# Block-sparse attention with a gated feed-forward on one Trainium2 core: the later Q, K, V casts move from GpSimd to ScalarE and VectorE, over one stage buffer

## The chip, the cores and the metric

The kernel runs on one core of one Trainium2 chip. The time is the device's, in microseconds (us): before the change the median of three runs is 315.1 us, from 315.01 to 315.33. TensorE is written PE in the profile, its weight loads PEld, VectorE is DVE, ScalarE is ACT, GpSimd is POOL, and SyncE, which here only issues transfers, is SP. A `q` behind an engine's name is its queue's sequencer.

## The reference

The inputs are q, k and v of 4 batches x 8 heads x 768 positions x 64, a list of 3 sampled key blocks for each of 24 query blocks, and the weights of a feed-forward layer from 512 to 1536 and back. All are fp32. The attention is masked by blocks of 32 positions; its output, with the heads side by side, is the input of a layer with an RMS norm and a SiLU gate.

```python
scores = scale * np.matmul(q, k.transpose(0, 1, 3, 2))
# a block pair is kept if |i - j| <= 1, if i or j is the first or last block,
# or if j is one of the three sampled blocks of i
scores = np.where(mask, scores, -1e9)
attn = softmax(scores)
x = np.matmul(attn, v)               # (4, 8, 768, 64) -> (3072, 512)
xn = x / rms(x) * rms_g
out = (silu(xn @ w_gate) * (xn @ w_val)) @ w_out
```

## The kernel before

**Tiling.** The 3072 positions are cut into 12 chunks of 256, three for each batch. Attention of a chunk is 12 tiles: four head pairs by three groups of 256 keys. A tile is four score matmuls (L556) into a PSUM bank pair `s`, one exponential on ScalarE into a third of the P buffer `pt` (L571), one multiplication with the 0/1 mask on VectorE (L578), and eight matmuls with V (L592). V has a column of ones behind it, so that these also give the softmax's denominator. A `pt` buffer holds the three tiles of one head pair, and there are four such buffers. In chunk 0 (`PEMASK`) the mask is added on TensorE instead (L562).

After a head pair VectorE divides by the denominator (`o_norm`, L604 and L606) into `x1`. After four pairs ScalarE sums squares (L615), GpSimd makes the reciprocal root (`rs`, L621 and L623), and VectorE scales into the bf16 `x2` (L628). The chunk must then be turned, so that its features lie on partitions, as `xn`. For chunks 0 and 11 this is done by eight transposes on TensorE and a copy from PSUM (`x_transposes` L638, `x_copy` L644). For chunks 1 to 10 (`XDMA`) it is two transposing DMAs on SP's queue (`x_dma`, L651).

The feed-forward of a chunk has six steps. In each, TensorE makes 256 columns of gate and of value for two feature tiles (`gp`, `vp`, L757), ScalarE takes a tanh (`th`, L763), and VectorE makes two products (`uu` L767, `hp` L774). Then TensorE multiplies with w_out (`yp`, L784), ScalarE copies the result (L801), and SP stores it (L802). The last ten steps take their PSUM banks from those that the scores had, and are called `gv`.

**How Q, K and V come in.** Batch 0's Q and K are cast to bf16 by the DMA or from small fp32 tiles, and transposed on TensorE. For batches 1 to 3, K, Q and V are loaded one after the other as fp32 into a `stage` tile of 1.5 MB (`load_stage`, L224, a DMA issued by GpSimd). There are two such tiles. GpSimd casts K and Q in six pieces of 512 columns each (`cast_c`, L229) and V in four pieces of 768 (`cast_v`, L234; batch 0's V too). The bf16 Q and K are then turned by transposing DMAs on SP's queue (L427), five for a batch, into `qkT`, from which the scores read.

**What sets the order.** No scheduler runs on the chip: each engine takes its instructions in the order in which they were emitted, and waits on semaphores. The order is made when the kernel is built, by a greedy planner (`Plan.run`, L50). Each task has the engines that may do it with a cost in us, the tasks that it depends on, buffers that it takes (`acq`) and gives back (`rel`), and a priority. At every step the planner takes the task with the smallest key, L98:

```python
key = (round(eager + wait + SOFT * t["prio"], 3), start + dur, t["seq"])
```

`wait` is `HOLD` for a task whose gate is closed. Only the scores have a gate: a score tile `i` is held while `i` is above `LEAD + SPEED * 144 * (share of feed-forward work done)`, and from tile 24 on, where tiles go in pairs, while the second `s` buffer isn't about to come free. A task that may run on two engines goes where its key is smaller. A transfer is reckoned as a share of one common DMA time, at L116, for the loads, and as a fixed latency for the transposing DMAs. The field `after` is a time before which the planner doesn't place a task; nothing in the emitted program enforces it. Loads of batch 2 have `after` 100, of batch 3 160.

Of the kernel before, what the change touches and what calls it, by code (L numbers as in the profile page):

```python
# [14 lines left out]
SEM = 0.06  # L15
START = dict(DVE=3.4, POOL=1.7, ACT=2.5, PE=4.4)
DMA0 = 3.0
HOLD = 0.2
SOFT = 0.0125
LEAD = 27  # L20
SPEED = 1.0
PRIO = {'av': 4, 'e': 10, 'g': 2, 'h': 6, 'm': 9, 'mk': 9, 'mt': -1, 'on': 3, 'rs': 2, 's': 2, 'sc': -12, 'sq': -7, 'th': -9, 'uu': 7, 'v': 4, 'x': 0, 'xt': -1, 'y': 7, 'yo': 1}


class Plan:
# [8 lines left out]
        self.tokens[name] = [0.0] * n  # L34

    def add(self, name, engines, fn, deps=(), prio=5, acq=(), rel=(), mode=None, lat=0.12,
            dma=None, after=0.0, gate=None, work=0.0):
        self.seq += 1
        assert name not in self.tasks, name
        self.tasks[name] = dict(  # L40
            name=name, engines=engines, fn=fn, deps=list(deps),
            prio=PRIO.get(name.split("_")[0].rstrip("0123456789"), prio), acq=list(acq),
            rel=list(rel), mode=mode, lat=lat, dma=dma, after=after, gate=gate, work=work,
            seq=self.seq)

    def soon(self, name, n):
# [3 lines left out]
    def run(self, log=None):  # L50
# [84 lines left out]
def kernel(  # L135
# [29 lines left out]
    const = ctx.enter_context(tc.tile_pool(name="const", bufs=1))  # L165
    raw = ctx.enter_context(tc.tile_pool(name="raw", bufs=1))
    qkpool = ctx.enter_context(tc.tile_pool(name="qkpool", bufs=2))
    ppool = ctx.enter_context(tc.tile_pool(name="ppool", bufs=4))
    xpool = ctx.enter_context(tc.tile_pool(name="xpool", bufs=2))
    work = ctx.enter_context(tc.tile_pool(name="work", bufs=2))  # L170
    ffw = ctx.enter_context(tc.tile_pool(name="ffw", bufs=3))
# [12 lines left out]
        return ps_f.tile([P, 512], FP32, name=name, tag="f")  # L184

    PEMASK = (0,)
    MAT = (0, 21.0, 32.0)
    QAT = (4.6, 20.0, 31.0)
    plan = Plan()
    for name, n in (("s", 2), ("o", 1), ("f", 3), ("pt", 4), ("x1", 2), ("x2", 3), ("xn", 3),  # L190
                    ("hp", 2), ("th", 3), ("uu", 3), ("yo", 3), ("qk", 2), ("raw", 1), ("sw", 8), ("stage", 2), ("t", 4)):
        plan.pool(name, n)

    kf = raw.tile([P, 2, NC * D], FP32, name="kf")
# [23 lines left out]

    stages = {}

    def load_stage(b, i):
        stages[b, i] = raw.tile([P, H, NC * D], FP32, name="stage", tag="stage", bufs=2)
        if b:
            nc.gpsimd.dma_start(out=stages[b, i], in_=(qv, kv, vv)[i][b])  # L224

    def cast_c(b, i, c):
        raw_tiles(b)
        flat = (qraw, kraw)[i][b].rearrange("p h w -> p (h w)")
        nc.gpsimd.tensor_copy(  # L229
            out=flat[:, c * DM:(c + 1) * DM].rearrange("p (h d) -> p h d", h=H),  # L230
            in_=stages[b, i][:, :, c * D:(c + 1) * D])

    def cast_v(b, pr):
        nc.gpsimd.tensor_copy(  # L234
            out=va[b % 2][:, 2 * pr:2 * pr + 2, :, 0:D],
            in_=stages[b, 2][:, 2 * pr:2 * pr + 2, :].rearrange("p h (c d) -> p h c d", c=NC))

    tid = const.tile([32, S], I32, name="tid")
# [74 lines left out]
    def act(n):  # L313
        return n / 1200.0 + 0.055
# [12 lines left out]
    def load_v0(lo):  # L327
        if lo == 0:
            load_stage(0, 2)
        nc.gpsimd.dma_start(out=stages[0, 2][:, lo:lo + 4, :], in_=vv[0, :, lo:lo + 4, :])  # L330
# [170 lines left out]
    for b in range(1, B):  # L501
        plan.add(f"rawq{b}", {"SP": 0.0}, lambda e: None, acq=["raw"], lat=0.0, prio=0,
                 deps=[f"raw{b - 1}"])
        for i in (1, 0, 2):
            swdge(f"l{b}_{i}", lambda b=b, i=i: load_stage(b, i), 4.4,
                  [">wo"] if (b, i) == (1, 1) else [">" + last], 20 + b, acq=["stage"],
                  after=0.0 if b == 1 else 60.0 * b - 20.0)
            last = f"l{b}_{i}"
            if i < 2:
                prev = None  # L510
                for c in range(NC):
                    plan.add(f"c{b}_{i}_{c}", {"POOL": 0.56}, lambda e, b=b, i=i, c=c: cast_c(b, i, c),
                             deps=[f"l{b}_{i}", f"rawq{b}"] + ([">" + prev] if prev else []),
                             rel=["stage"] if c == NC - 1 else [], prio=10)
# [109 lines left out]
        mss[ch] = rs  # L624

    def scale_x(ch, qt):
        x2s[ch, qt] = xpool.tile([P, DM], BF16, name="x2", tag="x2", bufs=3)
        nc.vector.scalar_tensor_tensor(  # L628
            out=x2s[ch, qt], in0=x1s[ch][:, qt].rearrange("p h d -> p (h d)"),
            scalar=mss[ch][:, qt:qt + 1], in1=gB, op0=ALU.mult, op1=ALU.mult)  # L630
# [9 lines left out]
                    in_=x2s[ch, qt][:, c * P:(c + 1) * P], identity=ident)  # L640

    def x_copy(e, ch):
        xns[ch] = xpool.tile([P, KC, CQ], BF16, name="xn", tag="xn", bufs=3)
        (nc.scalar.copy if e == "ACT" else nc.vector.tensor_copy)(  # L644
            out=xns[ch].rearrange("p c t -> p (c t)"),
            in_=xts[ch].rearrange("p c t -> p (c t)"))

    def x_dma(ch, qt):
        if qt == 0:
            xns[ch] = xpool.tile([P, KC, CQ], BF16, name="xn", tag="xn", bufs=3)  # L650
        nc.sync.dma_start_transpose(  # L651
            out=xns[ch][:, :, qt * P:(qt + 1) * P], in_=x2s[ch, qt])
# [53 lines left out]
    for ch in range(NCH):  # L706
# [178 lines left out]
```

## Time and profile before

| | |
|---|---|
| median of three runs | 315.1 us (315.01 to 315.33) |
| profiled execution: time, span | 314.4 us, 312.6 us |
| mean granted TensorE clock | 0.989 |
| busy: TensorE, VectorE, ScalarE, GpSimd | 291.9, 238.3, 214.4, 70.7 us |
| chain that ended last | TensorE 60%, VectorE 16%, DMA 8%, ScalarE 7%, GpSimd 5% |
| moved by DMA | 36.68 MB, mean 117 GB/s |

The span runs from the first to the last instruction of one profiled execution; its own time is 1.8 us longer. Busy times are unions of instruction records, and a matmul's record is longer than its share of the pipeline. "<-" behind a group of instructions names what ended the idle time before it. The columns of each view are told where it is shown.

### The profile page before, as it was taken

Reading aid. Unit: us, or ns where it says so; the run is one execution under the profiler, and the core shown is the slowest. Engines: PE = TensorE matmul, PEld = TensorE weight load, DVE = VectorE, ACT = ScalarE, POOL = GpSimd, SP = SyncE. Lnnn points to the kernel's source line nnn. Section 1 sums busy time; section 2 is a strip of 40 time slices with the busy share of each in tenths; the row PEclk is TensorE's granted clock in tenths of the full one; section 3 lists DMA queues with packets and bytes.
Section 4 is the critical chain, followed back from the end, with each engine's and each line's share of the span. In section 5 each row is a group of like instructions: output and inputs, shape, how many; then the busy total and the mean of one; then the engine's idle time right before and its main releaser. Section 6 shows DMA issues by size and latency. Waiting matters only on the chain.

```text
span 312.6 us, 7944 instructions
## 1 busy us (share of the span) xinstructions
PE 291.9 (93%) x3358; PEld 204.3 (65%) x3358; DVE 238.3 (76%) x439; ACT 214.4 (69%) x302; POOL 70.7 (23%) x108
## 2 busy tenths in 40 slices
PE   7697997799999497999999999999999999999995
PEld 2475675477757274875775875876866867858682
DVE  6238999779959478786996998887887887866361
ACT  4979997458797385767786776787787777733231
POOL 9551009350021009431002409420010010010000
PEclk9999999799999889999999999999999999999999
DMA  8999995893009702992107915954003003000001
GB/s 124 293 209 209 208 359 147 258 145 76 0 37 291 182 2 67 272 168 67 37 2 241 293 24 157 235 66 103 2 3 101 2 2 101 3 36 34 35 34 67
DMA packets 44135, 36.68 MB, mean 117 GB/s; under 512 B 31364, under 2 KB 37652, under 8 KB 44100
## 3 DMA queue, kind: packets, MB, share of 16 engines
q0 software_dynamic: 9984, 21.76, 27.5%
q1 hardware_dynamic: 33700, 14.16, 20.9%
q8 instruction: 26, 0.43, 0.6%
q10 hardware_dynamic: 416, 0.26, 0.3%
q14 instruction: 9, 0.07, 0.1%
HBM read 28.57 MB, written 6.29 MB: 112 GB/s over the span
## 4 chain that ended last, share of the span: by engine, by line
PE 60%; DVE 16%; DMA 8%; ACT 7%; POOL 5%; issue 4%; POOLq 0%; ACTq 0%; DVEq 0%
PE yp L784 14%; PE gp L757 13%; PE vp L757 12%; DVE pt L578 6%; PE gv L757 4%; DVE x L628 4%; DMA stage<-in_v_dram 4%; DMA xn<-x 4%; ACT junk L615 3%; ACT pt L571 3%; DVE uu L767 2%; DVE hp L774 2%; POOL rs L623 2%; DVE x L606 2%; ACT th L763 1%
## 5 line engine op out<-in xcount | busy, mean ns | idle before, releaser
L578 DVE TENSOR_TENSOR pt<-pt,Mk 128x1024 bf16<-128x1024 bf16 x132 | 94.5, 742 | 3.9 <-ACT pt L571 3.8
L784 PE MATMUL yp<-wo,hp 128*128 128x512 bf16 x288 | 71.5, 384 | 0.7 <-DVE hp L774 0.7
L757 PE MATMUL gp<-xn,wg 128*128 128x256 bf16 x512 | 67.3, 275 | 4.6 <-DMA xn<-x 4.6
L757 PE MATMUL vp<-xn,wv 128*128 128x256 bf16 x512 | 69.2, 272 | 0.1
L757 PEld LDWEIGHTS <-wg 128*128 128x128 bf16 x576 | 56.3, 98 | 14.3 <-DMA xn<-x 4.8
L592 PEld LDWEIGHTS <-pt 128*128 128x128 bf16 x1152 | 45.9, 98 | 28.3 <-DVE pt L578 11.1
L763 ACT ACTIVATE th<-gp 128x512 bf16<-128x512 f32 x64 | 38.2, 597 | 37.4 <-PE gp L757 37.1
L767 DVE SCALAR_TENSOR_TENSOR uu<-th,gp 128x512 bf16<-128x512 bf16 x64 | 43.6, 682 | 19.2 <-ACT th L763 18.9
L757 PEld LDWEIGHTS <-wv 128*128 128x128 bf16 x576 | 51.8, 97 | 6.5 <-issue 1.1
L774 DVE TENSOR_TENSOR hp<-uu,vp 128x512 bf16<-128x512 bf16 x64 | 43.7, 682 | 2.8 <-PE vp L757 0.2
L621 POOL TENSOR_SCALAR rs<-ms 128x2 f32<-128x2 f32 x12 | 2.8, 231 | 180.4 <-ACT junk L615 180.4
L784 PEld LDWEIGHTS <-hp 128*128 128x128 bf16 x288 | 25.8, 98 | 24.4 <-issue 2.4
L556 PEld LDWEIGHTS <-qkT 64*128 64x128 bf16 x576 | 23.6, 94 | 20.2 <-issue 16.8
L801 ACT ACTIVATE yo<-yp 128x512 f32<-128x512 f32 x23 | 13.7, 597 | 26.3 <-PE yp L784 26.3
L628 DVE SCALAR_TENSOR_TENSOR x<-x,rs,gB 128x512 bf16<-128x512 f32 x24 | 19.2, 840 | 12.7 <-POOL rs L623 12.6
L234 POOL CAST va<-stage 128x768 bf16<-128x768 f32 x16 | 14.3, 928 | 15.8 <-DMA stage<-in_v_dram 15.8
L615 ACT ACTIVATE junk<-x 128x512 bf16<-128x512 f32 x24 | 15.0, 629 | 3.2 <-DVE x L606 3.1
L229 POOL CAST kb<-stage 128x512 bf16<-128x512 f32 x18 | 13.9, 812 | 5.8 <-DMA stage<-in_k_dram 5.8
L229 POOL CAST qb<-stage 128x512 bf16<-128x512 f32 x18 | 12.4, 734 | 0.0
L767 DVE SCALAR_TENSOR_TENSOR uu<-th,gv 128x512 bf16<-128x512 bf16 x8 | 5.5, 688 | 7.2 <-ACT th L763 7.2
L763 ACT ACTIVATE th<-gv 128x512 bf16<-128x512 f32 x8 | 4.8, 597 | 8.3 <-PE gv L757 8.3
L623 POOL TENSOR_TENSOR rs<-rs,nhalf 128x2 f32<-128x2 f32 x12 | 8.6, 715 | 1.0
(515 smaller groups left out, 391.9 us busy)
## 6 DMA issues: line engine op xcount, KB each, us to landing
out_dram<-yo SPq DMA_DIRECT2D x23, 256.0 KB, 2.4
stage<-in_k_dram POOLq DMA_DIRECT2D x3, 1536.0 KB, 7.8
stage<-in_q_dram POOLq DMA_DIRECT2D x3, 1536.0 KB, 12.5
stage<-in_v_dram POOLq DMA_DIRECT2D x3, 1536.0 KB, 9.6
stage<-in_v_dram POOLq DMA_DIRECT2D x2, 768.0 KB, 11.0
wg<-in_moe_w_gate_dram POOLq DMA_DIRECT2D x2, 768.0 KB, 19.5
wv<-in_moe_w_val_dram POOLq DMA_DIRECT2D x2, 768.0 KB, 22.5
wo<-in_moe_w_out_dram POOLq DMA_DIRECT2D x1, 1536.0 KB, 30.5
```

The costliest lines, as they stand in the source:

```text
L229: nc.gpsimd.tensor_copy(out=flat[:, c * DM:(c + 1) * DM].rearrange("p (h d) -> p h d", h=H), in_=stages[b, i][:, :, c * D:(c + 1) * D])
L556: nc.tensor.matmul(out=s_[:, e, jj * CQ:(jj + 1) * CQ], lhsT=x[rows, 1, 2 * j2 + jj, pr, :], rhs=x[rows, 0, 2 * ic:2 * ic + 2, pr, :], sta ...
L578: nc.vector.tensor_tensor(out=pv, in0=pv, in1=m.unsqueeze(1).to_broadcast([P, 2, 2 * CQ]), op=ALU.mult)
L592: nc.tensor.matmul(out=o_[:, qt, e, 0:D + 1], lhsT=pt[:, j2, e, jj * CQ + qt * P:jj * CQ + (qt + 1) * P], rhs=va[(ch // NIC) % 2][:, 2 * p ...
L615: nc.scalar.activation(out=junk, in_=x1s[ch][:, qt].rearrange("p h d -> p (h d)"), func=AF.Square, scale=float(DM) ** -0.5, accum_out=mss[ ...
L623: nc.gpsimd.tensor_tensor(out=rs, in0=rs, in1=nhalf, op=ALU.pow)
L628: nc.vector.scalar_tensor_tensor(out=x2s[ch, qt], in0=x1s[ch][:, qt].rearrange("p h d -> p (h d)"), scalar=mss[ch][:, qt:qt + 1], in1=gB, ...
L757: nc.tensor.matmul(out=pp[:, half * CQ:(half + 1) * CQ], lhsT=w[:, c, f * P:(f + 1) * P], rhs=xns[u][:, c, :], start=(c == 0), stop=(c == ...
L763: nc.scalar.activation(out=ths[u, fp], in_=gst[u, fp, "gp"], func=AF.Tanh, scale=0.5)
L767: nc.vector.scalar_tensor_tensor(out=uus[u, fp], in0=ths.pop((u, fp)), scalar=1.0, in1=gst.pop((u, fp, "gp")), op0=ALU.add, op1=ALU.mult)
L774: nc.vector.tensor_tensor(out=hps[u][:, 2 * fp:2 * fp + 2, :].rearrange("p f t -> p (f t)"), in0=uus.pop((u, fp)), in1=gst.pop((u, fp, "vp ...
L784: nc.tensor.matmul(out=yst[u, t], lhsT=hps[u][:, f, t * P:(t + 1) * P], rhs=wo[:, f, :], start=(f == 0), stop=(f == NF - 1))
```

## The change

It has seven parts.

- The casts of Q and K of batches 1 to 3 (36 of 512 columns) and all V casts (16 of 768) may run on ScalarE or VectorE, and no longer on GpSimd.
- There is one `stage` tile instead of two, so that a load waits for the last cast of the one before it. Each load is issued as two halves of four heads, and the first two V casts wait for the first half alone.
- There are five P buffers instead of four, and four each of `x2` and `xn` instead of three.
- Chunk 1's x is transposed on TensorE, as chunk 0's is (`XFROM = 2`).
- The planner reckons the transposing DMAs as DMA time in line with the loads, and adds 2 us (`XSLACK`) to the landing of an x.
- `HOLD` goes from 0.2 to 4303.634, `LEAD` from 27 to 22, `SPEED` from 1.0 to 1.05.
- `SOFT` goes from 0.0125 to 0.0025, and the priorities are new.

```diff
-HOLD = 0.2
-SOFT = 0.0125
-LEAD = 27
-SPEED = 1.0
-PRIO = {'av': 4, 'e': 10, 'g': 2, 'h': 6, 'm': 9, 'mk': 9, 'mt': -1, 'on': 3, 'rs': 2, 's': 2, 'sc': -12, 'sq': -7, 'th': -9, 'uu': 7, 'v': 4, 'x': 0, 'xt': -1, 'y': 7, 'yo': 1}
+HOLD = 4303.634
+SOFT = 0.0025
+LEAD = 22
+SPEED = 1.05
+PRIO = {'av': 10, 'e': -30, 'g': -51, 'h': -11, 'm': 30, 'mk': 25, 'mt': 4, 'on': 6, 'rs': 42, 's': 2, 'sc': 23, 'sq': -7, 't': 3, 'th': -63, 'uu': 2, 'v': 14, 'x': 7, 'xt': 11, 'y': 22, 'yo': -15}
...
                 dma_free = max(dma_free, end + 0.5) + t["dma"]
-                fin = dma_free + 1.6
+                fin = dma_free + 1.6 + t["extra"]
...
-    ppool = ctx.enter_context(tc.tile_pool(name="ppool", bufs=4))
+    ppool = ctx.enter_context(tc.tile_pool(name="ppool", bufs=5))
...
+    def copy(e, out, in_):
+        (nc.scalar.copy if e == "ACT" else nc.vector.tensor_copy)(out=out, in_=in_)
+
     def load_stage(b, i):
-        stages[b, i] = raw.tile([P, H, NC * D], FP32, name="stage", tag="stage", bufs=2)
-        if b:
-            nc.gpsimd.dma_start(out=stages[b, i], in_=(qv, kv, vv)[i][b])
+        stages[b, i] = raw.tile([P, H, NC * D], FP32, name="stage", tag="stage", bufs=1)
+
+    def load_part(b, i, lo, hi):
+        nc.gpsimd.dma_start(out=stages[b, i][:, lo:hi, :], in_=(qv, kv, vv)[i][b, :, lo:hi, :])
...
-        plan.add(f"va0_{pr}", {"POOL": 0.8}, lambda e, pr=pr: cast_v(0, pr),
+        plan.add(f"va0_{pr}", {"DVE": 0.5, "ACT": act(768)}, lambda e, pr=pr: cast_v(e, 0, pr),
...
-            swdge(f"l{b}_{i}", lambda b=b, i=i: load_stage(b, i), 4.4,
-                  [">wo"] if (b, i) == (1, 1) else [">" + last], 20 + b, acq=["stage"],
-                  after=0.0 if b == 1 else 60.0 * b - 20.0)
+            plan.add(f"sta{b}_{i}", {"SP": 0.0}, lambda e, b=b, i=i: load_stage(b, i), acq=["stage"],
+                     lat=0.0, prio=0,
+                     deps=[">wo"] if (b, i) == (1, 1) else [">" + last] + ([cast] if b > 1 else []),
+                     after=0.0 if b == 1 else 60.0 * b - 20.0)
+            for lo in (0, 4):
+                swdge(f"l{b}_{i}_{lo}", lambda b=b, i=i, lo=lo: load_part(b, i, lo, lo + 4), 2.2,
+                      [">" + last], 20 + b)
...
-                    plan.add(f"c{b}_{i}_{c}", {"POOL": 0.56}, lambda e, b=b, i=i, c=c: cast_c(b, i, c),
+                    plan.add(f"c{b}_{i}_{c}", {"ACT": act(512), "DVE": 0.42},
+                             lambda e, b=b, i=i, c=c: cast_c(e, b, i, c),
...
-                    plan.add(f"va{b}_{pr}", {"POOL": 0.8}, lambda e, b=b, pr=pr: cast_v(b, pr),
+                    plan.add(f"va{b}_{pr}", {"ACT": act(768), "DVE": 0.55},
...
-            plan.add(f"dt{b}_{i}_{c0}", {"SP": 0.3 + 1.25 * (c1 - c0)},
+            plan.add(f"dt{b}_{i}_{c0}", {"SP": 1.5},
-  ... lat=2.5, prio=1)
+  ... dma=1.1 * (c1 - c0), prio=1)
...
-        x2s[ch, qt] = xpool.tile([P, DM], BF16, name="x2", tag="x2", bufs=3)
+        x2s[ch, qt] = xpool.tile([P, DM], BF16, name="x2", tag="x2", bufs=4)
-        xns[ch] = xpool.tile([P, KC, CQ], BF16, name="xn", tag="xn", bufs=3)
+        xns[ch] = xpool.tile([P, KC, CQ], BF16, name="xn", tag="xn", bufs=4)
...
-    XDMA = range(1, NCH - 1)
+    XFROM = 2
+    XDMA = range(XFROM, NCH - 1)
+    XSLACK = 2.0
...
-                plan.add(f"xd{ch}_{qt}", {"SP": 1.5}, lambda e, ch=ch, qt=qt: x_dma(ch, qt),
+                plan.add(f"xd{ch}_{qt}", {"SP": 1.25}, lambda e, ch=ch, qt=qt: x_dma(ch, qt), dma=1.1, extra=XSLACK,
```

More of the change, by code (lines that the diff above doesn't have):

```diff
@@ L36, in add @@
     def add(self, name, engines, fn, deps=(), prio=5, acq=(), rel=(), mode=None, lat=0.12,
-            dma=None, after=0.0, gate=None, work=0.0):
+            dma=None, after=0.0, gate=None, work=0.0, extra=0.0):
         self.seq += 1
@@ L42, in add @@
             prio=PRIO.get(name.split("_")[0].rstrip("0123456789"), prio), acq=list(acq),
-            rel=list(rel), mode=mode, lat=lat, dma=dma, after=after, gate=gate, work=work,
+            rel=list(rel), mode=mode, lat=lat, dma=dma, after=after, gate=gate, work=work, extra=extra,
             seq=self.seq)
@@ L186 @@
     PEMASK = (0,)
+    CPRIO = 6
     MAT = (0, 21.0, 32.0)
@@ L189 @@
     plan = Plan()
-    for name, n in (("s", 2), ("o", 1), ("f", 3), ("pt", 4), ("x1", 2), ("x2", 3), ("xn", 3),
-                    ("hp", 2), ("th", 3), ("uu", 3), ("yo", 3), ("qk", 2), ("raw", 1), ("sw", 8), ("stage", 2), ("t", 4)):
+    for name, n in (("s", 2), ("o", 1), ("f", 3), ("pt", 5), ("x1", 2), ("x2", 4), ("xn", 4),
+                    ("hp", 2), ("th", 3), ("uu", 3), ("yo", 3), ("qk", 2), ("raw", 1), ("sw", 8), ("stage", 1), ("t", 4)):
         plan.pool(name, n)
@@ L219, with cast_c, cast_v @@
     stages = {}
+    def copy(e, out, in_):
+        (nc.scalar.copy if e == "ACT" else nc.vector.tensor_copy)(out=out, in_=in_)
     def load_stage(b, i):
-        stages[b, i] = raw.tile([P, H, NC * D], FP32, name="stage", tag="stage", bufs=2)
-        if b:
-            nc.gpsimd.dma_start(out=stages[b, i], in_=(qv, kv, vv)[i][b])
-    def cast_c(b, i, c):
+        stages[b, i] = raw.tile([P, H, NC * D], FP32, name="stage", tag="stage", bufs=1)
+    def load_part(b, i, lo, hi):
+        nc.gpsimd.dma_start(out=stages[b, i][:, lo:hi, :], in_=(qv, kv, vv)[i][b, :, lo:hi, :])
+    def cast_c(e, b, i, c):
         raw_tiles(b)
         flat = (qraw, kraw)[i][b].rearrange("p h w -> p (h w)")
-        nc.gpsimd.tensor_copy(
-            out=flat[:, c * DM:(c + 1) * DM].rearrange("p (h d) -> p h d", h=H),
+        copy(
+            e, out=flat[:, c * DM:(c + 1) * DM].rearrange("p (h d) -> p h d", h=H),
             in_=stages[b, i][:, :, c * D:(c + 1) * D])
-    def cast_v(b, pr):
-        nc.gpsimd.tensor_copy(
-            out=va[b % 2][:, 2 * pr:2 * pr + 2, :, 0:D],
+    def cast_v(e, b, pr):
+        copy(
+            e, out=va[b % 2][:, 2 * pr:2 * pr + 2, :, 0:D],
             in_=stages[b, 2][:, 2 * pr:2 * pr + 2, :].rearrange("p h (c d) -> p h c d", c=NC))
@@ L329, in load_v0 @@
             load_stage(0, 2)
-        nc.gpsimd.dma_start(out=stages[0, 2][:, lo:lo + 4, :], in_=vv[0, :, lo:lo + 4, :])
+        load_part(0, 2, lo, lo + 4)
     def load_g():
@@ L509 @@
+            last = f"sta{b}_{i}"
+            for lo in (0, 4):
+                swdge(f"l{b}_{i}_{lo}", lambda b=b, i=i, lo=lo: load_part(b, i, lo, lo + 4), 2.2,
+                      [">" + last], 20 + b)
+                last = f"l{b}_{i}_{lo}"
+            loaded = [f"l{b}_{i}_0", f"l{b}_{i}_4"]
             if i < 2:
-                prev = None
+                cast = None
                 for c in range(NC):
-                    plan.add(f"c{b}_{i}_{c}", {"POOL": 0.56}, lambda e, b=b, i=i, c=c: cast_c(b, i, c),
-                             deps=[f"l{b}_{i}", f"rawq{b}"] + ([">" + prev] if prev else []),
-                             rel=["stage"] if c == NC - 1 else [], prio=10)
-                    prev = f"c{b}_{i}_{c}"
+                    plan.add(f"c{b}_{i}_{c}", {"ACT": act(512), "DVE": 0.42},
+                             lambda e, b=b, i=i, c=c: cast_c(e, b, i, c),
+                             deps=loaded + [f"rawq{b}"] + ([">" + cast] if cast else []),
+                             rel=["stage"] if c == NC - 1 else [], prio=CPRIO)
+                    cast = f"c{b}_{i}_{c}"
@@ L516 @@
             else:
                 for pr in range(NP):
-                    plan.add(f"va{b}_{pr}", {"POOL": 0.8}, lambda e, b=b, pr=pr: cast_v(b, pr),
-                             deps=[f"l{b}_2", f"one{b % 2}"] + ([f">va{b}_{pr - 1}"] if pr else [])
+                    plan.add(f"va{b}_{pr}", {"ACT": act(768), "DVE": 0.55},
+                             lambda e, b=b, pr=pr: cast_v(e, b, pr),
+                             deps=[loaded[pr // 2], f"one{b % 2}"] + ([f">va{b}_{pr - 1}"] if pr else [])
@@ L520 @@
                              + ([f"av{(b - 2) * NIC + NIC - 1}_{NP - 1}_2"] if b >= 2 else []),
-                             rel=["stage"] if pr == NP - 1 else [], prio=10)
+                             rel=["stage"] if pr == NP - 1 else [], prio=CPRIO)
+                cast = f"va{b}_{NP - 1}"
         plan.add(f"qk{b}", {"SP": 0.0}, lambda e: None, deps=[f"rawq{b}"], acq=["qk"], lat=0.0,
@@ L525 @@
         for i, c0, c1 in KT:
-            plan.add(f"dt{b}_{i}_{c0}", {"SP": 0.3 + 1.25 * (c1 - c0)},
+            plan.add(f"dt{b}_{i}_{c0}", {"SP": 1.5},
                      lambda e, b=b, i=i, c0=c0, c1=c1: transposes_dma(b, i, c0, c1),
-                     deps=[f"qk{b}"] + ([">" + prev] if prev else []) + [f"c{b}_{i}_{c}" for c in range(c0, c1)], lat=2.5, prio=1)
+                     deps=[f"qk{b}"] + ([">" + prev] if prev else []) + [f"c{b}_{i}_{c}" for c in range(c0, c1)], dma=1.1 * (c1 - c0), prio=1)
             prev = f"dt{b}_{i}_{c0}"
@@ L649, in x_dma @@
         if qt == 0:
-            xns[ch] = xpool.tile([P, KC, CQ], BF16, name="xn", tag="xn", bufs=3)
+            xns[ch] = xpool.tile([P, KC, CQ], BF16, name="xn", tag="xn", bufs=4)
         nc.sync.dma_start_transpose(
             out=xns[ch][:, :, qt * P:(qt + 1) * P], in_=x2s[ch, qt])
-    XDMA = range(1, NCH - 1)
+    XFROM = 2
+    XDMA = range(XFROM, NCH - 1)
+    XSLACK = 2.0
     SPT = {}
```

1 line of the change is left out of this document (removed).

## The prediction

> **What bounds the kernel now.** I read the page first, for the busy shares, then the busy time by stage, TensorE's waits, the rows around each wait, and last the chain in order of time.
>
> ```profile
> span 312.6 us, 7944 instructions
> PE 291.9 (93%) x3358; PEld 204.3 (65%) x3358; DVE 238.3 (76%) x439; ACT 214.4 (69%) x302; POOL 70.7 (23%) x108
> ```
> ```profile
> core 0: us, PE busy (x) PEld busy (x) DVE busy (x) ACT busy (x) POOL busy (x), PEclk, DMA share, GB/s
> 0.00:30.00 30.00, 23.80 (x359) 14.89 (x361) 15.54 (x51) 23.29 (x32) 16.59 (x31) 1.00 1.07 209
> 50.00:60.00 10.00, 6.19 (x53) 2.92 (x51) 9.96 (x13) 3.67 (x5) 7.05 (x11) 0.83 0.79 213
> 100.00:110.00 10.00, 5.45 (x55) 4.03 (x52) 5.36 (x11) 3.84 (x6) 0.00 (x0) 0.88 0.72 199
> 120.00:130.00 10.00, 8.42 (x101) 5.48 (x98) 8.02 (x14) 6.18 (x8) 7.94 (x12) 1.00 0.64 178
> 130.00:300.00 170.00, 169.12 (x1882) 121.66 (x1880) 135.65 (x239) 116.75 (x168) 25.53 (x37) 1.00 0.36 85
> ```
> The columns are each engine's busy time with its instructions, then the granted clock and the DMA. From 130 us to 300 TensorE is idle for 170 - 169.12 = 0.88 us: the end is set by how much of its work is left at 130. Its total idle time is 312.6 - 291.9 = 20.7 us, and 3.8 of it lies in 50 to 60, 4.55 in 100 to 110, 1.6 in 120 to 130 and 6.2 in the first 30. Only these can be won, with the two stretches at a lowered clock (0.83 and 0.88). The view of waits names them:
>
> ```profile
> PE gp L757 <- DMA xn<-x: 4.6, 1, 4.6
> PE o__1059 L592 <- DVE pt L578: 3.1, 2, 2.7
> PE o__342 L592 <- POOL va L234: 1.9, 1, 1.9
> ```
>
> **The stall at 54 us** is VectorE's. The timeline there:
>
> ```profile
> 53.51 5.00 DVE L578 TENSOR_TENSOR pt<-pt,Mk 128x1024 bf16<-128x1024 bf16 x3
> 53.51 3.84 POOL L229 CAST qb<-stage 128x512 bf16<-128x512 f32 x6
> 56.95 0.62 PE L592 MATMUL o__1059<-va,pt 128*128 128x65 bf16 x8 [2.71 <-DVE pt L578]
> ```
> Mask multiplications, grouped for 53 to 58 us and then for 130 to 160 us:
> ```profile
> L578 DVE TENSOR_TENSOR pt<-pt,Mk x3: 678/1091/3381, 53.5 to 57.8; 128x1024 bf16<-128x1024 bf16 x3
> ...
> L578 DVE TENSOR_TENSOR pt<-pt,Mk x16: 681/684/693, 131.0 to 159.1; 128x1024 bf16<-128x1024 bf16 x16
> ```
> One multiplication that takes 0.68 us elsewhere took 3.38 and ended with GpSimd's six casts; the next took 1.09. That is 2.7 + 0.4 = 3.1 us of VectorE lost to GpSimd. Right after the stall six output matmuls took 2.47 us on the chain, elsewhere 1.29: 1.2 us more at the lowered clock.
>
> ```profile
> 57.57 2.47 PE yp L784 x6
> ...
> 84.25 1.29 PE yp L784 x6
> ...
> 215.82 0.87 PE gp L757 x8
> ...
> 238.35 0.87 PE gp L757 x8
> ```
>
> **The stall at 103 us** is a transposing DMA's, chunk 3's x. GpSimd, SP and TensorE in the timeline, then the landings of stage and of xn in 93 to 108 us:
>
> ```profile
> 92.33 0.72 POOL L623 TENSOR_TENSOR rs<-rs,nhalf 128x2 f32<-128x2 f32 x1
> 93.01 0.95 POOL L224 DMA_DIRECT2D stage<-in_k_dram  x1
> 93.96 0.88 POOL L224 DMA_DIRECT2D stage<-in_q_dram  x1
> ...
> 93.90 1.20 SPq L651 DMA_TRANSPOSE xn<-x  x1
> 96.02 1.53 SPq L651 DMA_TRANSPOSE xn<-x  x1
> ...
> 107.86 1.86 PE L757 MATMUL gp<-xn,wg 128*128 128x256 bf16 x8 [4.55 <-DMA xn<-x]
> ```
> ```profile
> DMA to landing us min/median/max: 7.8/10.1/12.4
> ...
> DMA to landing us min/median/max: 13.1/13.1/13.1
> ```
> The planner's `after` of 100 us for batch 2's loads holds nothing on the chip: GpSimd runs into them right behind chunk 3's rs. K (7.8 us) and Q (12.4) go out back to back, so Q lands at 93.96 + 12.4 = 106.3, and x, issued between them, at 93.90 + 13.1 = 107.0: after both. The median of all twenty x is 2.4.
>
> ```profile
> xn<-x SPq DMA_TRANSPOSE x20, 2.4
> ```
>
> **The change part by part.** The sum is made against the profiled execution, 314.4 us (span 312.6 and 1.8 around it); the median of the runs is 315.1, 0.7 above. The rows for the prices, grouped by line and form:
>
> ```profile
> L234 POOL CAST va<-stage 128x768 bf16<-128x768 f32 x16 | 14.3, 928 | 15.8 <-DMA stage<-in_v_dram 15.8
> L229 POOL CAST kb<-stage 128x512 bf16<-128x512 f32 x18 | 13.9, 812 | 5.8 <-DMA stage<-in_k_dram 5.8
> L763 ACT ACTIVATE th<-gp 128x512 bf16<-128x512 f32 x64 | 38.2, 597 | 37.4 <-PE gp L757 37.1 <-ACT pt L571 0.3
> L477 DVE TENSOR_SCALAR Mk<-mp 128x512 bf16<-128x512 f32 x5 | 3.3, 682 | 0.0
> L401 DVE COPY qkT<-tq 128x512 bf16<-128x512 bf16 x5 | 2.1, 423 | 0.5 <-PE tq L395 0.3
> L638 PE MATMUL xT<-ident,x 128*128 128x128 bf16 x16 | 1.6, 221 | 1.0 <-DVE x L628 1.0
> L330 POOL DMA_DIRECT2D stage<-in_v_dram x2 | 1.5, 778 | 0.0
> ```
> *Price of a cast.* No cast of a stage from SBUF runs on VectorE or ScalarE here. For 512 columns VectorE lies between 0.42 (the copy) and 0.68 (the fp32 source); I take 0.5. ScalarE: 0.6. For 768 I take half as much again, 0.8.
>
> *(a) K and Q of batch 1.* Twelve casts leave GpSimd, so the 3.1 us stretch of the masks goes, but six casts of about 0.5, 3.0 us, come onto VectorE, which was busy 9.96 of 10 us there; ScalarE had 6.3 us free and can take the others. VectorE's balance is about even, so I count back not the whole loss (3.8 idle + 1.2 clock = 5.0) but 4.0; bounds 1.5 and 5.0.
>
> *(b) One stage, halves, x by slack.* Q's load now waits for K's last cast, so only K can stand ahead of chunk 3's x: 93.0 + 7.8 = 100.8, x 0.7 behind it as now (107.0 against 106.3), its second piece about 0.6 later: 102.1, before the 103.3 at which TensorE ran out. But TensorE gets there earlier by (a). If attention of chunk 3 moves up with it nothing of the stall is left, if not 4.0 - 1.2 = 2.8. I leave 1.3: of 4.55 idle and 1.3 clock (1.86 against 0.87 for eight gp matmuls, and an estimated 0.3 for those behind them) 4.6 is won; bounds 0 and 5.9.
>
> Does attention move up? Batch 1's chain, K cast, Q load, Q cast, V load, is now serial:
>
> ```profile
> 47.48 4.78 POOL L229 CAST kb<-stage 128x512 bf16<-128x512 f32 x6
> 52.56 0.95 POOL L224 DMA_DIRECT2D stage<-in_v_dram  x1 [0.30 <-POOL kb L229]
> 62.22 3.11 POOL L234 CAST va<-stage 128x768 bf16<-128x768 f32 x3 [4.87 <-DMA stage<-in_v_dram]
> ...
> L556 PE MATMUL s__1322<-qkT x4: 269/274/279, 70.8 to 70.9; 64*128 64x256 bf16 x4
> ```
> K's casts 47.5 to 50.5 (six of 0.5 in a row), Q's load about 9.7 as V's from 52.56 to 62.22, to 60.2, casts to 63.2, transposes about 2.4 later: scores of batch 1 from some 66 us, against 70.8. V's halves land by 73, and the fifth P buffer holds exponentials until then. So it can.
>
> *(c) Batch 2's K casts* at 120 us likewise: 1.0 of the 1.6 idle; bounds 0 and 1.6. *(d) V0:* its cast held the first value matmul; VectorE, idle there (15.5 busy of 30), saves 0.3; bounds 0 and 0.8.
>
> *(e) Chunk 1's x on TensorE* adds eight transposes. Sixteen took 1.6 with 1.0 of waiting, so 0.8 with its mode change, and 1.3 with all the waiting; bounds 0.4 and 1.3. The copy from PSUM goes to ScalarE or VectorE, covered as the casts are. Two DMAs leave SP, ahead of K's transposes; that gain I leave at zero.
>
> *(f) Casts queued on the wrong engines.* 52 casts, 36 of about 0.55 and 16 of 0.8, are 33 us on two engines that have 74 + 98 us idle. What counts is waiting: GpSimd waited 15.8 + 5.8 us for loads at its casts, where only rs was queued behind. On ScalarE exponentials and tanh stand behind them, on VectorE masks and hp, and TensorE waits for all four. Below: nothing, where the plan's landing is late enough. Above: half of those waits, 9.8 us without V0's 2.0. The planner puts casts where it expects the landing and now counts transposes into the DMA's time, so I take 0.8.
>
> *(g) Eighteen load issues for nine:* 18 x 0.78 = 14.0 us, against nine of 0.88 to 0.95, some 5.8 us more on GpSimd, 23% busy: nothing. If rs stood behind two, 1.6 us on one x. *(h) New weights, LEAD, HOLD:* from 130 us on nothing can be won but 0.88; the chain above repeats every 22.53 us there (215.82, 238.35). HOLD now bars scores beyond LEAD altogether, yet 22 tiles plus 12.6 per finished chunk leave each chunk's attention about a chunk (22.5 us) ahead of its use, with the steps from the last score to x and the 13.1 of the worst x to fit in. I take 0; bounds -0.9 and +2.
>
> Sum: -4.0 - 4.6 - 1.0 - 0.3 + 0.8 + 0.8 = -8.3. 314.4 - 8.3 = 306.1, and on the runs' scale 306.8 us.
>
> The Trainium skill speaks against casting on VectorE: "SBUF — State Buffer", section "SBUF: two separate sides", says that an fp32 copy within SBUF there can lock GpSimd out, so that it cannot write DMA descriptors until the copy ends. No run so far has such a copy beside a load issue. It is the third rival below.
>
> **Rivals.** *x still late (0.17).* Attention of chunk 3 gains nothing from (a) while TensorE does, or another load falls in front of x. For it: K's load of batch 2 still goes out right behind rs. Against: Q's no longer can. (b) gives nothing: 306.8 + 4.6 = 311.4.
>
> *Slower: load waits on ScalarE and VectorE (0.21).* A cast stands at the head of a queue while its load is under way. K of batch 2 landed 7.8 us after issue, V of batch 1 9.7; the code plans 0.85 + 0.5 + 4.4 + 1.6 = 7.35 for two halves. With 9.8 us of waiting on the path instead of 0.8, and two stalls that lower the clock at 1.2 each, the time is 306.8 + 9.0 + 2.4 = 318.2. It decides from 8.3 us of such waiting. Against it: from 130 us VectorE is idle a fifth of the time (135.65 of 170), and there a short wait is covered.
>
> *GpSimd held off by the new copies (0.05).* Each of batch 1's six half-load issues waits for one cast of 0.5: V, and with it chunk 3's x, 3.0 us later: 309.8. The page's lock would do this.
>
> *The stalls only move (0.07).* VectorE stays the bound of 50 to 60 and x comes too late by as much as TensorE gains: about 315.
>
> **How the numbers follow.** The forecast has 0.50, its own range 302 (all upper bounds: -5.0 - 5.9 - 1.6 - 0.8 - 0.9 + 0.4 = -13.8, from 315.1, is 301) to 310. To hold 8 in 10 the range reaches into the slower case: 301.5 to 318. The runs of before lie within 0.32 us, so 0.2% (0.6 us) can be told. Faster: 0.50 + 0.17 + 0.05 = 0.72; same: most of the last rival, 0.06; slower 0.22.
>
> **What would show it.** Right: no mask multiplication above 1.1 us; no idle time of 2 us before a value matmul at 50 to 60; chunk 3's x landing within about 9 us; TensorE saturated from about 115 instead of 130, with the same 22.5 us per chunk. Wrong: ScalarE or VectorE idle before a cast for "DMA stage", several us in sum; GpSimd's load issues well above 0.78; a gap of TensorE for xn at 90 to 110; or a chunk spacing above 22.5.

## The result and the profile after

The changed kernel takes 306.17 us (median of four), against 315.22 before: ratio 0.9694, 95% interval 0.9645 to 0.9742. Timed again later it took 307.27 (median of six, 304.30 to 309.79), ratio 0.9708 (0.9668 to 0.9748). The forecast was 306.8. The execution profiled with the first timing was the longest of its four, 313.1 us, so the rows below are those of the second timing's profile (span 304.0 us) where nothing else is said. An execution more than 1.5% above the fastest of its kernel counts as a slow one here: medians and ranges hold such executions, the ratios leave them out.

Busy time by stage after the change, columns as before:

```profile
core 0: us, PE busy (x) PEld busy (x) DVE busy (x) ACT busy (x) POOL busy (x), PEclk, DMA share, GB/s
0.00:30.00 30.00, 26.11 (x351) 15.81 (x352) 17.95 (x55) 23.19 (x32) 13.17 (x27) 1.00 1.06 209
50.00:60.00 10.00, 9.86 (x115) 6.76 (x114) 9.71 (x20) 8.52 (x13) 1.55 (x2) 1.00 0.84 143
60.00:100.00 40.00, 38.08 (x415) 26.59 (x413) 29.98 (x54) 30.03 (x47) 4.96 (x8) 1.00 0.52 118
100.00:110.00 10.00, 9.94 (x124) 6.48 (x121) 7.38 (x16) 8.87 (x11) 0.00 (x0) 1.00 0.71 232
120.00:130.00 10.00, 9.54 (x109) 5.11 (x107) 8.95 (x21) 7.72 (x10) 0.54 (x1) 1.00 1.14 160
130.00:300.00 170.00, 169.21 (x1880) 121.80 (x1876) 136.04 (x249) 120.99 (x176) 12.10 (x22) 1.00 0.33 86
```
The holes at 50 to 60, 100 to 110 and 120 to 130 are gone, and the clock stands at 1.00 in all these stages. A new hole of 1.9 us has come in 60 to 100. From 130 us TensorE is saturated as it was.

Where the time came from shows when TensorE's work is counted. The table adds up the gp, vp and gv matmuls begun by then at 0.109 us, the yp at 0.215, the value matmuls at 0.0375 and the scores at 0.054. These are prices from the chains (0.87 for eight, 1.29 for six, 0.60 for sixteen), that of a score an estimate from four at a spacing of about 0.22.

| by | before | changed | ahead |
|---|---|---|---|
| 50 us | 28.1 | 27.9 | -0.2 |
| 60 us | 32.2 | 36.6 | 4.4 |
| 80 us | 51.5 | 53.4 | 1.9 |
| 100 us | 70.4 | 72.7 | 2.3 |
| 120 us | 83.7 | 91.6 | 7.9 |
| 130 us | 91.6 | 100.5 | 8.9 |
| 290 us | 245.6 | 254.4 | 8.9 |

The stall at 54 us gives 4.4 us and more than half of it is lost again by 80. The stall at 103 gives 5.6. After 130 nothing more comes.

The masks, grouped over the whole span, and then ScalarE's timeline at 49 us:

```profile
L592 DVE TENSOR_TENSOR pt<-pt,Mk x132: 677/683/694, 27.9 to 262.1; 128x1024 bf16<-128x1024 bf16 x132
```
```profile
49.30 3.20 ACT L223 CAST kb<-stage 128x512 bf16<-128x512 f32 x6
```
No mask multiplication takes more than 0.694 us; before, one took 3.38. All six K casts of batch 1 went to ScalarE; its Q casts too.

The loss by 80 us. ScalarE, then TensorE, then the stage landings in 52 to 55 us, then the first scores of batch 1:

```profile
67.56 1.14 ACT L223 CAST qb<-stage 128x512 bf16<-128x512 f32 x2 [1.86 <-DMA stage<-in_q_dram]
68.60 0.59 ACT L779 ACTIVATE th<-gp 128x512 bf16<-128x512 f32 x1
```
```profile
69.96 1.03 PE L773 MATMUL vp<-xn,wv 128*128 128x256 bf16 x8 [1.17 <-DVE uu L783]
```
```profile
DMA to landing us min/median/max: 8.3/11.1/13.9
```
```profile
L570 PE MATMUL s__1399<-qkT x4: 269/274/279, 74.8 to 74.9; 64*128 64x256 bf16 x4
```
Q's second half landed 13.9 us after its issue. ScalarE stood 1.86 us at the cast that waits for it, with a tanh queued behind, and through `uu` that held up a vp for 1.17 us. The scores of batch 1 begin at 74.8 us, before at 70.8.

Chunk 3's x. GpSimd, SP, the landings of xn in 98 to 108 us, and TensorE:

```profile
98.24 1.56 POOL L229 DMA_DIRECT2D stage<-in_k_dram  x2
...
99.11 2.94 SPq L665 DMA_TRANSPOSE xn<-x  x2
```
```profile
DMA to landing us min/median/max: 6.1/6.5/6.9
```
```profile
97.72 1.89 PE L800 MATMUL yp<-wo,hp 128*128 128x512 bf16 x8
...
100.77 1.46 PE L800 MATMUL yp<-wo,hp 128*128 128x512 bf16 x6
...
103.46 1.89 PE L800 MATMUL yp<-wo,hp 128*128 128x512 bf16 x8
...
105.83 0.67 PE L606 MATMUL o__1944<-va,pt 128*128 128x65 bf16 x16
106.55 1.03 PE L773 MATMUL gp<-xn,wg 128*128 128x256 bf16 x8
```
x lands 6.1 to 6.9 us after issue instead of 13.1. But it is issued 5 us later, so chunk 3's first gp starts at 106.55, only 1.3 us earlier than before (107.86). What differs is that chunk 2's 24 output matmuls now run while x is under way. There is nothing to spare: TensorE was done with the work in front at 106.50, and x's second piece landed at 106.51. Before, the output matmuls stood behind that gp, the first at 115:

```profile
115.33 1.03 PE L784 MATMUL yp<-wo,hp 128*128 128x512 bf16 x4
```

### The profile page after: what moved, and what is told of

Same layout as the page of the kernel before. It is cut to its first block, busy times and chain, and to the rows that moved or that the text cites. A ratio compares the mean times of both kernels' runs of the same rounds, so it can differ in the third digit from the quotient of the medians.

```text
span 311.3 us, 7965 instructions
## 1 busy us (share of the span) xinstructions
PE 295.6 (95%) x3366; PEld 207.2 (67%) x3366; DVE 240.2 (77%) x466; ACT 226.9 (73%) x328; POOL 36.2 (12%) x65
## 4 chain that ended last, share of the span: by engine, by line
PE 73%; DVE 11%; DMA 9%; ACT 3%; issue 1%; POOL 1%; DVEq 0%; ACTq 0%
PE yp L800 17%; PE vp L773 14%; PE gp L773 14%; DMA qkT<-kb 6%; PE gv L773 4%; DVE pt L592 4%; DMA xn<-x 3%; DVE hp L790 2%; DVE uu L783 2%; ACT pt L585 1%; DMA qf<-in_q_dram 1%; DVE x L620 1%; PE tq L400 1%; DVE x L642 1%; ACT junk L629 1%
## 5 line engine op out<-in xcount | busy, mean ns | idle before, releaser
L592 DVE TENSOR_TENSOR pt<-pt,Mk 128x1024 bf16<-128x1024 bf16 x132 | 86.7, 684 | 4.8 <-ACT pt L585 4.6
L773 PE MATMUL vp<-xn,wv 128*128 128x256 bf16 x512 | 71.2, 274 | 0.5 <-DVE uu L783 0.5
L800 PE MATMUL yp<-wo,hp 128*128 128x512 bf16 x288 | 70.0, 379 | 0.0
L773 PEld LDWEIGHTS <-wg 128*128 128x128 bf16 x576 | 56.6, 99 | 13.9 <-DMA xn<-x 3.2
L642 DVE SCALAR_TENSOR_TENSOR x<-x,rs,gB 128x512 bf16<-128x512 f32 x24 | 17.3, 748 | 5.0 <-POOL rs L637 4.7
L406 DVE COPY qkT<-tq 128x256 bf16<-128x256 bf16 (+2 forms) x11 | 4.4, 412 | 7.8 <-PE tq L400 7.6
L229 POOL DMA_DIRECT2D stage<-in_v_dram x8 | 6.2, 778 | 29.0 <-DVE qb L223 15.3
L229 POOL DMA_DIRECT2D stage<-in_q_dram x6 | 4.5, 759 | 37.3 <-ACT kb L223 22.4
## 6 DMA issues: line engine op xcount, KB each, us to landing
qb<-in_q_dram POOLq DMA_DIRECT2D x1, 512.0 KB, 13.9
```

The costliest lines, as they stand in the source:

```text
L229: nc.gpsimd.dma_start(out=stages[b, i][:, lo:hi, :], in_=(qv, kv, vv)[i][b, :, lo:hi, :])
L592: nc.vector.tensor_tensor(out=pv, in0=pv, in1=m.unsqueeze(1).to_broadcast([P, 2, 2 * CQ]), op=ALU.mult)
L642: nc.vector.scalar_tensor_tensor(out=x2s[ch, qt], in0=x1s[ch][:, qt].rearrange("p h d -> p (h d)"), scalar=mss[ch][:, qt:qt + 1], in1=gB, ...
L773: nc.tensor.matmul(out=pp[:, half * CQ:(half + 1) * CQ], lhsT=w[:, c, f * P:(f + 1) * P], rhs=xns[u][:, c, :], start=(c == 0), stop=(c == ...
L800: nc.tensor.matmul(out=yst[u, t], lhsT=hps[u][:, f, t * P:(t + 1) * P], rhs=wo[:, f, :], start=(f == 0), stop=(f == NF - 1))
```

## The experiments

**1. The changed kernel again.** No edit.

> The changed kernel once more, unaltered, for a profile of an ordinary execution (that of the first profile took 313.1 us, the other three 304.7 to 306.9). Theory (two stalls gone): 305 to 307 us; no idle time of TensorE above 1.5 us in 50 to 60, at most some 2 us before xn at 100 to 110, and the wait of 3.85 us at 131 (VectorE's Q casts of batch 2 behind a load that landed 16 us after its issue) shorter or gone. Rival (load waits sit on VectorE and ScalarE in every execution): the wait at 131 is there again with 3 us or more, and the time lies near 313.

307.27 us, just above the theory's range. In the profiled execution (305.79 us) TensorE's gap at that place, now 129.8 us, is 0.46 us, and none from 50 to 60 is above 0.25. The rival falls for this execution. Its wait is real in one place all the same, at 67 us (above).

**2. The casts on GpSimd, in the changed kernel's order.**

```diff
     def copy(e, out, in_):
-        (nc.scalar.copy if e == "ACT" else nc.vector.tensor_copy)(out=out, in_=in_)
+        nc.gpsimd.tensor_copy(out=out, in_=in_)
```

> The changed kernel in its own order, but all 52 casts are emitted on GpSimd, in the places that they have there. Theory (GpSimd's casts stretch VectorE's masks): masks above 1.0 us are back, the stretch costs VectorE 3 to 5 us, TensorE idles again at 50 to 60, and the time is 308 to 311. Rival (the planner's new order makes the gain): within 1 us of the changed kernel, 305 to 307. Rival (ScalarE and VectorE pay for the casts): faster than the changed kernel, 303 to 305.

312.16 us (307.26 to 315.44), above the ranges of all three accounts, ratio 0.9807 (0.9744 to 0.9871). The stretched masks are back; minimum, median and maximum of 132, in ns:

```profile
L592 DVE TENSOR_TENSOR pt<-pt,Mk x132: 675/684/1304, 27.2 to 263.7; 128x1024 bf16<-128x1024 bf16 x132
```
The two intervals just touch (0.9744 and 0.9748), so GpSimd is probably the worse place, by about 1%. TensorE idles 1.1 us in 50 to 60, not 3.8: with one mask of 1.09 us in that stage and none of 3.38, little of the old stall returns. All masks together take 6.3 us more than in the changed kernel, where 3 to 5 were forecast. The profiled execution is the quickest of the four, 307.26 us, so where the others lose time isn't seen.

**3. Only the casts, in the order of before.** Even pieces on VectorE, odd ones on ScalarE.

```diff
+    def copy(n, out, in_):
+        (nc.scalar.copy if n % 2 else nc.vector.tensor_copy)(out=out, in_=in_)
...
-        nc.gpsimd.tensor_copy(
+        copy(c,
```

> The kernel before in its own order, but each of the 52 casts is emitted on VectorE (even pieces) or ScalarE (odd pieces) in place of GpSimd; two stage tiles as before. Theory: the stretched masks are gone, the wait of 2.71 us at 54 with its lowered clock goes, the x wait at 103 stays or grows a little as TensorE comes earlier; 310 to 312 us. Rival (the casts wait for their loads at the head of ScalarE's and VectorE's queues): those engines idle 5 us or more before casts, 315 to 320.

317.29 us, ratio 1.006 (1.0029 to 1.0091): slower by 0.6%. The rival's account holds: VectorE and ScalarE stand 6.4 and 2.8 us at V casts whose loads are under way, and the time lies in its range. TensorE's waits:

```profile
PE gp L762 <- DMA xn<-x: 5.5, 1, 5.5
PE gp L762 <- DVE hp L779: 2.9, 2, 2.2
PE o__342 L597 <- DVE va L227: 1.7, 1, 1.7
PE warm L266 <- DVE idle L246: 1.2, 1, 1.2
PE xT L643 <- DVE x L633: 1.0, 3, 0.6
PE o__1059 L597 <- DVE pt L583: 1.0, 2, 0.7
```
The stall at 54 went from 2.7 to 0.7 us as the theory has it. The wait for xn took over (4.6 to 5.5), and a new one, 2.2 us for VectorE's hp, came at 200.6 us, right behind 2.4 us in which VectorE stood at a V cast of batch 3.

**4. Only the single stage.** Casts on GpSimd, loads whole, planned anew.

```diff
-                    ("hp", 2), ("th", 3), ("uu", 3), ("yo", 3), ("qk", 2), ("raw", 1), ("sw", 8), ("stage", 2), ("t", 4)):
+                    ("hp", 2), ("th", 3), ("uu", 3), ("yo", 3), ("qk", 2), ("raw", 1), ("sw", 8), ("stage", 1), ("t", 4)):
...
-        stages[b, i] = raw.tile([P, H, NC * D], FP32, name="stage", tag="stage", bufs=2)
+        stages[b, i] = raw.tile([P, H, NC * D], FP32, name="stage", tag="stage", bufs=1)
```

> The kernel before with one stage tile in place of two, planned anew with its own numbers; casts stay on GpSimd, loads stay whole. Theory: Q of batch 2 no longer goes out beside K, so chunk 3's x lands within 9 to 10 us of its issue instead of 13 and the wait of 4.6 us at 103 shrinks to under 2; the stretch of the masks stays; 310 to 312 us. Rival (the stall only moves, since batch 1's chain of loads and casts becomes serial): scores of batch 1 start later than 75 us and the time is 314 to 318.

324.52 us, ratio 1.0264 (1.0220 to 1.0307). Theory and rival were both short of it. From its waits:

```profile
POOL va L234 <- DMA stage<-in_v_dram: 24.8, 5, 9.2
POOL qb L229 <- DMA stage<-in_q_dram: 17.4, 2, 9.3
...
PE gp L757 <- DMA xn<-x: 5.3, 2, 3.2
...
PE o__3663 L592 <- POOL va L234: 3.1, 1, 3.1
...
PE o__2534 L592 <- POOL va L234: 2.2, 1, 2.2
```
With one stage the chain of loads and casts is serial, and V comes last: TensorE waits for V's casts of batches 2 and 3, and still for xn. Chunk 3's x did land 8.3 us after its issue, as the theory has it. But it was issued 4.8 us later than before, at 98.68 us, so that it landed at 106.99 (before 107.04), and TensorE waited 3.2 us for it. Batch 1's scores begin at 70.9 us, so the loss doesn't lie where the rival put it.

**5. Chunk 2's output matmuls ahead of chunk 3's gp, nothing else.**

```diff
+            if f == 0 and u == 3:
+                deps.append(f">y{u - 1}_1_{YP - 1}")
```

> The kernel before with one more order given to the planner: chunk 3's first gp may come only after the last output matmul of chunk 2. All else as before. New theory (x isn't early, TensorE has other work): x lands as late as before, 13 us after issue, but chunk 2's 24 output matmuls (5.2 us) now lie ahead of the wait, so the 4.6 us at 103 shrink to under 1 and the clock stays up; 310 to 312 us. Rival (x must land earlier): the wait stays above 3 us and the time at 315.

311.18 us, ratio 0.9882 (0.9835 to 0.9929). The landings of xn in 94 to 110 us, and the busy time of two stages:

```profile
DMA to landing us min/median/max: 13.2/13.2/13.2
```
```profile
50.00:60.00 10.00, 6.16 (x54) 3.12 (x52) 9.93 (x14) 4.31 (x5) 7.71 (x11) 0.90 0.80 216
...
100.00:110.00 10.00, 10.00 (x135) 6.58 (x130) 8.60 (x18) 8.21 (x11) 0.00 (x0) 1.00 0.87 247
```
x is as late as it ever was, and TensorE doesn't wait for it: x landed at 108.29 us, and chunk 3's first gp begins at 113.19. Order alone gives 4.8 us by the medians and 1.2% by the ratio, which is somewhat over half of the gain by the one and two fifths by the other. An earlier landing isn't needed.

**6. Experiments 3 and 5 together.** Both edits.

> The same order, with the 52 casts emitted on VectorE and ScalarE in turn. Alone, these casts made the kernel no faster (317.3 against 315.6), as the wait for xn grew from 4.6 to 5.5 us. Theory (the two stalls hide each other): together they win more than each alone, 307 to 310. Rival (casts on these engines cost as much as the stretch of the masks): no faster than the run with the order alone, 310 to 313.

312.40 us, ratio 0.9869 (0.9831 to 0.9908), the same as 5. The theory falls and the rival holds: with the x wait gone, moving all 52 casts in turn still gains nothing.

**7. No slack for x.**

```diff
-    XSLACK = 2.0
+    XSLACK = 0.0
```

> The changed kernel with XSLACK 0 in place of 2. Theory (the slack keeps other work of TensorE ahead of each x): waits for xn come back, 1 to 3 us at one or more chunks, 308 to 311. Rival (the slack does nothing, the DMA time now counted for the transposes is enough): 305 to 307.5.

313.44 us, above the ranges of both accounts, ratio 0.9871 (0.9800 to 0.9942). In the profile, of an execution of 315.23 us, the wait is back:

```profile
PE gp L773 <- DMA xn<-x: 3.6, 1, 3.6
PE yp L800 <- DVE hp L790: 3.5, 2, 3.3
```
The first wait is chunk 3's, but not because its gp stands ahead of other work: all 24 output matmuls of chunk 2 lie in front of it here too. TensorE was done with them at 104.96 us, 1.5 us earlier than in the changed kernel, and x landed at 108.50, 2.0 us later. So this run doesn't show that the slack is what moves those matmuls. The order was planned anew, and the second wait, at 153 us, may have other reasons.

**8. The old planner numbers.** PRIO too is that of the kernel before.

```diff
-HOLD = 4303.634
-SOFT = 0.0025
-LEAD = 22
-SPEED = 1.05
+HOLD = 0.2
+SOFT = 0.0125
+LEAD = 27
+SPEED = 1.0
```

> The changed kernel with the HOLD, SOFT, LEAD, SPEED and priorities of the kernel before. Theory (the moved casts, the single stage and the planner's count of the transposes make the gain): 306 to 309. Rival (the new numbers make most of it): 312 or more.

310.12 us, ratio 0.9857 (0.9805 to 0.9908), between the two accounts. By the ratios the rest of the change gives about half of the gain (1.4% of 2.9 to 3.1), by the medians about two thirds; the new numbers give what is left.

**9. Slack for the loads too.**

```diff
+    LSLACK = 3.0
...
-                      [">" + last], 20 + b)
+                      [">" + last], 20 + b, extra=LSLACK if b > 1 else 0.0)
```

> The changed kernel with 3 us added to the planner's landing of every half-load of batches 2 and 3, as XSLACK does for an x. Theory (the changed kernel's spread of 304 to 313 us comes from casts at the head of VectorE's and ScalarE's queues when a load lands late): the spread shrinks to 3 us and the median falls from 307.3 to 304 or 305. Rival (the spread has another cause): as wide as before, median 306 to 309.

310.20 us (305.39 to 313.07), above both accounts' ranges, and the spread is as wide as before. In the profile (309.25 us) no cast of batches 2 and 3 waits for its load; VectorE's longest such wait, 3.2 us at 17.8 us, is for V of batch 0, which got no slack. TensorE's longest wait, 3.0 us at 137.75 us (`vp` for `uu`), has no load in it either: VectorE made six Q casts in a row (2.10 us) and the scaling of x before that `uu`. So the theory finds no support, but how the other five executions spent their time isn't seen.

**10. On top of 5, only batch 1's K and Q casts, on ScalarE.**

```diff
     def cast_c(b, i, c):
...
-        nc.gpsimd.tensor_copy(
+        (nc.scalar.copy if b == 1 else nc.gpsimd.tensor_copy)(
```

> The kernel before with chunk 2's output matmuls ahead of chunk 3's gp (311.2 us by itself), and of the casts only batch 1's twelve of Q and K moved, to ScalarE, where the changed kernel has them. Theory (term (a) of the prediction, the stretched masks at 54 us): the wait of 2.71 us and its lowered clock go, 4.0 us are won, 306.5 to 308.5. Rival (what TensorE wins there it loses again in waiting later, as all 52 casts in turn showed no gain over 311.2): 310 to 312.

309.60 us, ratio 0.9832 (0.9801 to 0.9864): 1.6 us under experiment 5 by the medians and the ratios, just under the second account's range. The two intervals overlap, so that even this isn't certain. Two stages here, and the same two of experiment 5:

```profile
50.00:60.00 10.00, 9.21 (x105) 5.83 (x104) 6.72 (x13) 10.00 (x17) 0.95 (x1) 1.00 0.67 154
60.00:80.00 20.00, 17.93 (x182) 12.63 (x179) 15.50 (x28) 13.89 (x22) 4.42 (x6) 0.91 0.65 135
```
```profile
50.00:60.00 10.00, 6.16 (x54) 3.12 (x52) 9.93 (x14) 4.31 (x5) 7.71 (x11) 0.90 0.80 216
60.00:80.00 20.00, 19.73 (x222) 14.98 (x221) 15.68 (x28) 13.39 (x20) 4.09 (x6) 0.97 0.54 104
```
TensorE gains 3.05 us of busy time from 50 to 60 and loses 1.8 from 60 to 80. By the count of matmuls it is 3.6 us ahead at 60 and 0.7 at 80.

**11. Chunk 1's x by DMA again.**

```diff
-    XFROM = 2
+    XFROM = 1
```

> The changed kernel with chunk 1's x turned by DMA again. Theory (term (e): eight transposes cost 0.8 us, and the two DMAs only stood ahead of K's transposes): within 1.5 us of the changed kernel, 305.5 to 308.5, if anything faster. Rival (the DMAs in front of K's transposes hold up batch 1): 309 or more.

319.33 us, ratio 1.0133 (1.0090 to 1.0177): worse than before the change, and 12 us behind the changed kernel. TensorE's waits:

```profile
PE gp L773 <- DMA xn<-x: 1.9, 1, 1.9
PE o__3639 L606 <- DVE pt L592: 1.3, 1, 1.3
PE o__1925 L606 <- DVE pt L592: 1.3, 1, 1.3
PE o__1807 L606 <- DVE pt L592: 1.2, 1, 1.2
...
PE o__3587 L606 <- DVE pt L592: 1.1, 1, 1.1
```
The waits lie at 101 to 111 and 192 to 213 us, far from chunk 1, so the rival has the time right but not the reason. Two DMAs more in the planner's account gave another order throughout, and with the same numbers it came out a poor one. What the transposes are worth is not measured by this; in the changed kernel's profile 24 of them take 2.0 us, where 16 took 1.6.

**12. Four P buffers, three x2 and xn.**

```diff
-    ppool = ctx.enter_context(tc.tile_pool(name="ppool", bufs=5))
+    ppool = ctx.enter_context(tc.tile_pool(name="ppool", bufs=4))
```
and likewise 4 to 3 for x2 and xn, and in the planner's pools.

> The changed kernel with four P buffers and three each of x2 and xn again. Theory (batch 1's V lands only at 78 to 81 us, and the fifth buffer holds exponentials until then): attention of chunk 3 falls back by a head pair, 308 to 311. Rival (the buffers are never all in use): 305.5 to 308.

307.85 us (302.97 to 310.19), in the rival's range; the ratio on record is 0.9805 (0.9760 to 0.9850). The executions overlap with the changed kernel's, and the quickest of all on record, 302.97 us, is one of them. The ratio leans the theory's way, but two of the four, 302.97 and 307.39, average 0.9695 of the kernel before; it stays open. No version tried is faster than the changed kernel for certain.

## Why the prediction was right, point by point

The sum was -8.3; the medians fell by 9.05 us in the first timing and by 8.29 in the second. The two large terms came out near for reasons other than those given, and smaller errors cancel, so that it is partly luck that the sum is so close.

- **(a), 4.0.** The stretch went entirely, and by 60 us TensorE was 4.4 ahead. But at 80 it was 1.9, and batch 1's casts alone gain about 1.6, if anything (experiment 10); all 52 casts are worth about 1% in experiment 2 and nothing in 3 and 6. So no run shows the 4.0. The step that failed is that attention moves up ("So it can"): scores of batch 1 were forecast from 66 us and came at 74.8, as Q's load went out at 52.8 us and not at 50.5, and its second half landed at 67.46 and not at 60.2. "VectorE's balance is about even" was wrong too: all twelve casts went to ScalarE.
- **(b), 4.6.** The wait went, and 5.6 us came from 100 to 120. The latency was as worked out: x's second piece landed 8.3 us behind the load's issue (98.24 to 106.5; forecast 9.1). The failed step is that x would land at 102.1 us, before TensorE ran out of work. Chunk 3's attention came later, not earlier, so that x was issued at 99.11 us instead of 93.90 and landed at 106.5. What helped is that work had been moved: chunk 2's output matmuls. Experiment 5 shows that this is enough with x landing 13.2 us after its issue. Which part of the change moves them isn't shown: they lie ahead of the gp without the slack too (experiment 7), and 14 of the 24 do with the old numbers (experiment 8). That no wait is left is luck. TensorE had lost some 1.7 us at 67 to 73 us, see (f). In the execution of 313.1 us it hadn't: there it was done at 104.83 us, x landed at 106.95, and the wait was 2.16 us. The prediction never asked what stood behind the waiting gp in TensorE's queue, and the trace of before would have shown 24 yp matmuls from 115 us on.
- **(c), 1.0.** TensorE's idle time from 120 to 130 fell from 1.58 to 0.46.
- **(d), 0.3.** The wait of the first value matmul is gone, but by 30 us the work counted is 11.0, before 11.4: nothing came of it.
- **(e), 0.8.** The added matmuls took 0.4 and waited for nothing: the lower bound.
- **(f), 0.8.** ScalarE's wait of 1.86 us at Q's cast is the case of the second rival, at one load of nine. With the two waits of TensorE right behind it, it cost about 1.7 (1.17 and two of some 0.25): twice the 0.8. Little of it may have reached the end, since TensorE would otherwise have waited for x, see (b). The execution of 313.1 us had a dearer wait of this kind (see the last section).
- **(g)** The issues took 0.75 to 0.81 us each, nothing, as said. GpSimd held off by VectorE's fp32 copies, as the Trainium skill has it ("SBUF — State Buffer", section "SBUF: two separate sides"), would have lengthened them. That isn't seen, but no cast of a stage ran on VectorE beside a load's issue in this profile, so it wasn't tried.
- **(h), 0.** Experiment 8 puts the new numbers at about 3 us by the medians and 4.7 by the ratios, outside the bounds of -0.9 and +2. The step that failed is "nothing can be won but 0.88", which looked only behind 130 us: by the count of matmuls, experiment 8's profile is 4.4 us behind the changed kernel at 60 us and 3.2 at 130, so the numbers act early.

Of "x still late" the condition came true, not the price: x landed at 106.5 us, before at 107.0, but the order covered it. Experiments 4 and 11 came out slower than the kernel before, at 324.5 and 319.3 us: the one makes a single part of the change, the other leaves one out.

## What to carry to other kernels

When an in-order engine waits for a transfer, look first at what is queued behind the waiting instruction: work that could go ahead of it is often cheaper than an earlier landing. Parts of a planned change are not additive: two parts taken alone lost time here, and one part undone cost more than the whole had won. Where a part enters the planner, each run of it gives another order, and the part can't be told from the order. A cast moved to a busy engine brings its load's landing into that engine's queue.

## What was unexpected

A load and a transposing DMA that were under way together both took long. K's second transposing DMA of batch 1, issued at 52.55 us, and the second half of Q's load, issued at 53.60, landed at 64.84 and 67.46, after 12.3 and 13.9 us; the transposing DMA issued 1.6 us earlier landed in 4.1. The same pair of batch 2 took 14.8 and 11.8 us. What does it is open.

The changed kernel spreads more from execution to execution (304.3 to 309.8 in one series) than the kernel before (313.8 to 316.4) and the one of experiment 5 (310.6 to 312.2). One long execution can be read, that of 313.1 us. VectorE, then TensorE:

```profile
132.44 2.10 DVE L223 CAST qb<-stage 128x512 bf16<-128x512 f32 x6 [3.30 <-DMA qkT<-kb]
```
```profile
135.19 0.55 PE L606 MATMUL o__2340<-va,pt 128*128 128x65 bf16 x8 [3.85 <-DVE pt L592]
```
The second half of batch 2's Q load landed at 132.36 us, 16.3 us after its issue, and K's second transposing DMA, which the row names, at 132.39, after 17.4 us. In the other profile these casts began before that transposing DMA had landed, so it is the load that they wait for. VectorE stood 3.30 us with masks queued behind, and TensorE 3.85 for such a mask. By the count of matmuls this execution is 7.6 us ahead of the kernel before at 130 us and 2.2 at 140. That is the second rival's mechanism, "load waits on ScalarE and VectorE", in one execution. Whether it makes the spread of the others isn't shown: experiment 9 didn't find the cause, and it stays open.
